# RWKV-6 attention followed by a multiplicative FFN: all tables of a hand-scheduled kernel drawn anew

## The chip, the cores and the metric

The kernel runs on one core of a Trainium2 chip. The metric is the device time of one execution in microseconds (us); lower is better. The engines are named as in the profile: PE (TensorE, matrix products), PEld (its weight loads), DVE (VectorE), ACT (ScalarE), POOL (GpSimd), SP (SyncE, which here only issues transfers).

## The reference

Batch 4, 8 heads, 768 tokens, head size 48; then 3072 tokens of width 384 through a feed-forward block of width 1024 without a nonlinearity beside one product.

```python
state = zeros(B, H, D, D)
for t in range(S):
    cur = einsum('bhd,bhe->bhde', u[None] * k[:, :, t], v[:, :, t])
    y[:, :, t] = einsum('bhd,bhde->bhe', r[:, :, t], state + cur)
    state = w[:, :, t, :, None] * state + einsum('bhd,bhe->bhde', k[:, :, t], v[:, :, t])
x = y.transpose(0, 2, 1, 3).reshape(B * S, H * D)
a, b = x @ w1, x @ w2
out = ((a * b) @ w3) @ w_out
```

All inputs and the output are float32; the kernel's products run in bfloat16.

## The kernel before

**Units.** The 768 tokens are cut into six chunks of 128, the four batches into pairs. A unit is one chunk of one or two batches: units 0 and 1 are one batch each, units 2 to 12 two batches, thirteen in all. The recurrence becomes, inside a chunk, products of 128 x 128 matrices and, between chunks, a state of 48 x 48 per head that is carried along.

**Steps of a unit t.** `ln_t` takes the logarithm of w on ACT, `cs_t` sums it along the tokens (a product with a triangle of ones), `e_t`, `ne_t`, `iw_t` exponentiate it (ACT), `KRk_t`, `rw_t`, `KRr_t` scale k and r with it (DVE). `trk_t` and `trr_t` transpose the scaled k and r on PE (copied out of PSUM by `trke_t`, `trre_t`); units in the sets `DMA_K` and `DMA_R` have the transpose made by a DMA issued from SP instead (`dtk_t`, `dtr_t`). Units in `RAW` transpose the unscaled r (`trw_t`) and sum the logarithms a second time, transposed (`csT_t`, `et_t`, `KRw_t`). `m_t_b` is the score matrix of batch b (L552); it is masked either by one DVE multiplication (`msk_t_b`, L571) or, for the pairs in `POOL_MASK`, copied out by ACT (`mcp_t_b`, L558) and masked in SBUF by POOL or DVE (`maff_t_b`, L566, L564). `kv_t` makes the unit's addition to the state (L638), `T_t`, `S_t`, `Sb_t` carry the state on. `ys_t` is the state's part of y (L587), `yi_t_b` the part inside the chunk (L597). `rk_t`, `ruk_t`, `dg_t`, `dv_t` make the u term, and `yb_t` adds it (L603). `yt_t` transposes y on PE; for units in `DMA_Y` SP issues `dty_t_b` instead.

**Steps of the FFN.** Eight blocks prepare w3 @ w_out once: `wt_f_h` transposes w3 (L373), `w3Te_f` copies it out, `wm_f` multiplies by w_out (L382), `w34e_f` copies the block out. Only two buffers hold the transposed w3, so block f + 2 waits for block f. Then for each unit: `a_t_g` and `b_t_g`, 6 or 12 products into one PSUM bank (L679), `asb_t_g` copies a out (ACT, L684), `abT_t_g` multiplies it by b (DVE, L689), `o_t_b` makes 128 tokens of output (L695), `osb_t_b` copies them out, `st_t_b` stores them.

**Shapes of the products.** Most products on PE use all 128 rows and all 128 columns of the array. `m` and `ys` contract over the padded 64 elements of one head and use 64 rows, two heads taking the two halves in turn. `kv` writes 64 partitions of the output and uses 64 columns.

**Loads.** r, k and v are cast from float32 to bfloat16 by DMAs which POOL issues, in SBUF 192 KB for a unit of two batches (96 KB for one); w is loaded as float32 (384 KB, 192 KB). The weights go the same way: w3 in four parts of 512 KB, w_out (`wo`) 768 KB, w1 and w2 in two parts of 384 KB each. All these stand in POOL's own order, between its arithmetic. SP issues the first two loads of w.

**What sets the order.** Nothing is reordered by a scheduler: `ORDER` lists every step with its engine, and the last loop records them in that order. Each engine runs its own steps strictly in that order; `BANKS` names the PSUM bank and the buffer of each step. `warm7@8` issues eight products of zeros into bank 7; they serve no result.

```python
    with tc.manual_schedule():
        for e in ORDER.split():
            name, _, eng = e.partition("@")
            if name.startswith("warm"):
                warm(int(name[4:]), int(eng))
                continue
            steps[name](eng)
```

Of the kernel before, what the change touches and what calls it, by code (L numbers as in the profile page):

```python
# [48 lines left out]
tk0=0 m0_0=4,5 y0=4,5 yt0=1 kv0=2 a0_0=1 b0_0=0 a0_1=3 b0_1=3 o0_0=0 cs1=2 tr1=2 tk1=1 m1_0=0,1 y1=0,1 yt1=0 kv1=0
a1_0=0 b1_0=2 a1_1=1 b1_1=0 o1_0=4 cs2=4,5 ct2=0,1 tr2=6 tk2=7 m2_0=6,7 m2_1=1,2 y2=3,4 yt2=0 kv2=1 a2_0=5 b2_0=5  # L50
a2_1=2 b2_1=3 a2_2=4 b2_2=2 a2_3=0 b2_3=2 o2_0=5 o2_1=0 cs3=5,6 tr3=1 tk3=4 m3_0=1,2 m3_1=3,4 y3=3,4 yt3=1 kv3=6
a3_0=5 b3_0=0 a3_1=0 b3_1=3 a3_2=4 b3_2=4 a3_3=3 b3_3=0 o3_0=0 o3_1=7 cs4=6,7 tr4=1 tk4=5 m4_0=4,5 m4_1=3,4 y4=5,6
yt4=4 kv4=3 a4_0=0 b4_0=7 a4_1=1 b4_1=4 a4_2=5 b4_2=4 a4_3=1 b4_3=3 o4_0=3 o4_1=7 cs5=1,2 tr5=4 tk5=3 m5_0=1,2
m5_1=2,3 y5=5,6 yt5=4 kv5=7 a5_0=3 b5_0=6 a5_1=2 b5_1=3 a5_2=1 b5_2=3 a5_3=4 b5_3=3 o5_0=3 o5_1=7 cs6=1,2 ct6=6,7
tr6=7 tk6=0 m6_0=0,1 m6_1=2,3 y6=0,1 yt6=2 kv6=0 a6_0=7 b6_0=2 a6_1=7 b6_1=2 a6_2=0 b6_2=4 a6_3=7 b6_3=2 o6_0=4 o6_1=3
cs7=5,6 tk7=2 m7_0=5,6 m7_1=0,1 y7=5,6 kv7=1 a7_0=5 b7_0=1 a7_1=1 b7_1=4 a7_2=0 b7_2=0 a7_3=1 b7_3=0 o7_0=1 o7_1=1
cs8=1,2 tk8=3 m8_0=0,1 m8_1=0,1 y8=5,6 kv8=0 a8_0=2 b8_0=1 a8_1=2 b8_1=4 a8_2=3 b8_2=5 a8_3=4 b8_3=1 o8_0=0 o8_1=6
cs9=5,6 m9_0=2,3 m9_1=3,4 y9=2,3 kv9=0 a9_0=5 b9_0=3 a9_1=2 b9_1=1 a9_2=0 b9_2=3 a9_3=2 b9_3=0 o9_0=5 o9_1=6 cs10=0,1
# [17 lines left out]
trke_1@DVE ruk_0@POOL dg_1@DVE trre_1@ACT KRw_0@DVE w3_1@POOL dg_0@DVE m_1_0@PE cs_2@PE dv_1@POOL mcp_1_0@ACT kv_0@PE
trw_2@PE w3_2@POOL ne_2@ACT csT_2@PE maff_1_0@DVE vin_2@POOL wt_0_1@PE et_2@ACT m_0_0@PE KRk_2@DVE msk_0_0@DVE
trk_2@PE rk_2@POOL pc_2@ACT yi_1_0@PE trke_2@ACT KRw_2@DVE yi_0_0@PE w3Te_0@ACT S_0@DVE dv_0@POOL yb_1@DVE Sb_0@DVE
win_3@POOL yt_1@PE m_2_0@PE m_2_1@PE mcp_2_0@ACT wm_1@PE msk_2_1@DVE w3_3@POOL maff_2_0@POOL yb_0@DVE wm_0@PE
w1_1@POOL wt_3_0@PE w34e_0@ACT yt_0@PE w2_1@POOL wt_3_1@PE xT_1@ACT wt_2_0@PE w3Te_3@DVE wt_2_1@PE rin_3@POOL xT_0@DVE  # L80
wm_3@PE w3Te_2@DVE kin_3@POOL w34e_1@DVE wm_2@PE w34e_3@DVE vin_3@POOL wt_4_0@PE w34e_2@DVE wt_5_0@PE ruk_2@POOL
wt_4_1@PE yi_2_0@PE w3Te_4@DVE wt_5_1@PE kv_2@PE yi_2_1@PE ln_3@ACT S_2@DVE wm_4@PE win_4@POOL dg_2@DVE w3Te_5@ACT
cs_3@PE w1_0@POOL dv_2@DVE iw_3@ACT wm_5@PE e_3@ACT rin_4@POOL yb_2@DVE pc_3@ACT wt_6_0@PE w34e_4@DVE wt_7_0@PE
wt_6_1@PE wt_7_1@PE w3Te_6@DVE yt_2@PE w3Te_7@ACT w2_0@POOL a_0_1@PE xT_2@DVE a_1_1@PE a_2_3@PE b_2_3@PE kin_4@POOL
asb_2_3@ACT a_2_2@PE Sb_2@ACT abT_2_3@DVE asb_0_1@ACT win_5@POOL b_1_1@PE rw_3@DVE asb_1_1@ACT b_2_2@PE ne_3@ACT
KRr_3@DVE trr_3@PE win_6@POOL Sb_1@ACT KRk_3@DVE asb_2_2@ACT b_0_1@PE rk_3@DVE trre_3@ACT trk_3@PE ruk_3@DVE
vin_4@POOL wm_7@PE abT_2_2@DVE trke_3@ACT abT_0_1@DVE m_3_0@PE w34e_5@DVE w34e_7@ACT kv_3@PE kin_5@POOL m_3_1@PE
dg_3@DVE ln_4@ACT wm_6@PE mcp_3_0@ACT T_3@DVE dv_3@POOL msk_3_1@DVE cs_4@PE w34e_6@ACT a_0_0@PE iw_4@ACT rin_5@POOL
a_2_1@PE pc_4@ACT ne_4@ACT rw_4@DVE ys_3@PE vin_5@POOL e_4@ACT a_2_0@PE abT_1_1@DVE maff_3_0@DVE a_1_0@PE asb_2_0@ACT
KRr_4@DVE yi_3_1@PE win_7@POOL asb_1_0@ACT b_2_0@PE asb_0_0@ACT yi_3_0@PE abT_2_0@DVE b_0_0@PE rin_6@POOL KRk_4@DVE  # L90
trr_4@PE asb_2_1@ACT yb_3@DVE trk_4@PE b_1_0@PE rk_4@POOL trke_4@ACT trre_4@DVE b_2_1@PE abT_0_0@DVE ln_5@ACT m_4_0@PE
kin_6@POOL abT_2_1@DVE yt_3@PE mcp_4_0@ACT o_0_0@PE xT_3@DVE abT_1_0@DVE ln_6@ACT maff_4_0@POOL m_4_1@PE cs_5@PE
iw_5@ACT msk_4_1@DVE a_3_0@PE S_3@POOL ne_5@ACT csT_6@PE ruk_4@POOL kv_4@PE pc_6@ACT osb_0_0@ACT o_1_0@PE T_4@DVE
pc_5@ACT e_5@ACT rin_7@POOL dg_4@DVE et_6@ACT a_3_1@PE KRk_5@DVE cs_6@PE kin_7@POOL asb_3_0@ACT rk_5@DVE a_3_3@PE
asb_3_1@ACT rw_5@DVE ys_4@PE win_8@POOL asb_3_3@ACT b_3_3@PE ruk_5@DVE osb_1_0@ACT KRr_5@DVE trk_5@PE ne_6@ACT
abT_3_3@DVE yi_4_1@PE vin_6@POOL trr_5@PE dg_5@DVE kv_5@PE trre_5@ACT yi_4_0@PE o_2_1@PE dv_4@POOL trke_5@DVE ln_7@ACT
T_5@DVE m_5_0@PE dv_5@POOL iw_7@ACT trw_6@PE yb_4@DVE b_3_1@PE Sb_3@ACT yt_4@PE osb_2_1@ACT abT_3_1@DVE win_9@POOL
cs_7@PE mcp_5_0@ACT xT_4@DVE b_3_0@PE KRk_6@DVE pc_7@ACT e_7@ACT rin_8@POOL a_4_3@PE rk_6@DVE ne_7@ACT m_5_1@PE
abT_3_0@DVE a_3_2@PE win_10@POOL asb_4_3@ACT rw_7@DVE trk_6@PE asb_3_2@ACT S_4@DVE a_4_1@PE ln_8@ACT KRw_6@DVE
maff_5_0@POOL b_3_2@PE trke_6@DVE mcp_5_1@ACT vin_7@POOL ys_5@PE rk_7@DVE b_4_0@PE asb_4_1@ACT maff_5_1@DVE yi_5_0@PE  # L100
iw_8@ACT kv_6@PE kin_8@POOL Sb_4@DVE cs_8@PE T_6@DVE yi_5_1@PE abT_3_2@DVE pc_8@ACT b_4_3@PE ln_9@ACT S_5@POOL
yb_5@DVE a_4_0@PE ne_8@ACT vin_8@POOL b_4_1@PE Sb_5@DVE asb_4_0@ACT ruk_7@DVE a_4_2@PE e_8@ACT win_12@POOL ruk_6@DVE
o_3_0@PE abT_4_1@DVE abT_4_3@DVE kin_10@POOL asb_4_2@ACT KRk_7@DVE b_4_2@PE abT_4_0@DVE kv_7@PE m_6_1@PE abT_4_2@DVE
cs_9@PE mcp_6_1@ACT KRk_8@DVE yt_5@PE o_3_1@PE KRr_7@DVE pc_9@ACT ne_9@ACT rw_8@DVE osb_3_0@ACT T_7@DVE rk_8@POOL
trk_7@PE e_9@ACT dg_6@DVE st_3_0@SP m_6_0@PE st_2_1@SP trk_8@PE xT_5@ACT dtr_7@SP o_2_0@PE S_7@DVE trke_8@ACT
# [649 lines left out]
```

## Time and profile before

| | |
|---|---|
| time, 3 runs | 179.97, 180.78, 184.8 us; median 180.78 us |
| the profiled execution | 180.96 us, of which the span is 179.3 us and 1.66 us lie around it |
| busy share | PE 90%, DVE 74%, POOL 59%, ACT 55% |
| granted clock of PE, mean | 0.981 of full speed |
| bytes moved by DMA | 25.08 MB, 140 GB/s over the span |
| the chain that ended last | PE 53%, DVE 19%, DMA 10%, issue 6%, POOL 5%, ACT 3% |

The span runs from the first to the last instruction. The busy shares are averages over three stages: a start in which the weights arrive, a middle in which attention and FFN run beside each other, and an end with FFN alone. In a listing by time a row has the start, the length, the engine, the line and what was written from what; neighbours of one kind are merged (x18 is eighteen instructions). In square brackets stands the idle time before it and what ended that. Products overlap, so the length of a PE row reaches into the next one: what a row costs is the distance to the next row's start.

### The profile page before, as it was taken

What the parts mean: (1) busy time and instruction counts of PE and PEld (TensorE: products, weight loads), DVE (VectorE), ACT (ScalarE), POOL (GpSimd) and SP (SyncE); (2) the same over time, 40 slices, a digit from 0 to 9 for tenths busy, and PEclk for the clock granted to TensorE, in tenths of its full rate; (3) what the DMA queues carried; (4) which work ended last, traced back from release to release, by engine and by line L of the source; (5) the groups of instructions that cost most, each with busy time, mean ns of one, the idle gap of its engine ahead of it and who ended that gap; (6) DMA issues with size and microseconds to landing.
All of it is one profiled execution on the core that took longest, in us unless ns stands there. A gap on an engine that the chain in (4) does not pass through costs nothing.

```text
span 179.3 us, 4622 instructions
## 1 busy us (share of the span) xinstructions
PE 161.1 (90%) x1933; PEld 118.0 (66%) x1933; DVE 133.4 (74%) x207; ACT 98.7 (55%) x161; POOL 105.4 (59%) x99
## 2 busy tenths in 40 slices
...
GB/s 94 162 184 174 211 211 207 177 195 186 214 117 181 65 22 183 125 171 171 42 139 192 131 133 193 68 189 123 139 128 216 142 129 27 84 132 70 4 130 135
DMA packets 100423, 25.08 MB, mean 140 GB/s; under 512 B 92689, under 2 KB 98322, under 8 KB 100402
## 3 DMA queue, kind: packets, MB, share of 16 engines
...
## 4 chain that ended last, share of the span: by engine, by line
PE 53%; DVE 19%; DMA 10%; issue 6%; POOL 5%; ACT 3%; SPq 1%; POOLq 0%; DVEq 0%; ACTq 0%
PE banks L679 24%; PE banks L695 11%; PE banks L382 6%; DMA win<-in_w_dram 4%; DMA vin<-in_v_dram 3%; DMA xT<-yb 3%; PE banks L552 3%; DVE KR L446 2%; DVE KR L487 2%; DVE rk L521 2%; DVE rw L479 2%; PE banks L638 2%; PE banks L597 2%; DVE dg L531 2%; DVE w_bf L689 1%
## 5 line engine op out<-in xcount | busy, mean ns | idle before, releaser
L679 PE MATMUL banks<-xT,w_bf 128*128 128x256 bf16 (+1 forms) x624 | 70.9, 264 | 3.7 <-DMA xT<-yb 1.7
L679 PEld LDWEIGHTS <-w_bf 128*128 128x128 bf16 x624 | 54.7, 98 | 11.9 <-issue 4.7
L684 ACT COPY a_sb<-banks 128x512 f32<-128x512 f32 x48 | 27.8, 593 | 21.7 <-PE banks L679 19.8
L689 DVE TENSOR_TENSOR abT<-a_sb,banks 128x512 bf16<-128x512 f32 x28 | 18.8, 681 | 7.5 <-PE banks L679 6.1
L566 POOL TENSOR_SCALAR_AFFINE_SELECT Mbf<-Mbf 128x1024 bf16<-128x1024 bf16 x10 | 11.3, 1132 | 19.5 <-ACT Mbf L558 19.5
L695 PE MATMUL banks<-w,abT 128*128 128x384 bf16 x112 | 20.3, 326 | 0.0
L558 ACT CAST Mbf<-banks 128x1024 bf16<-128x1024 f32 x14 | 14.2, 1013 | 7.5 <-PE banks L552 7.5
L689 DVE TENSOR_TENSOR w_bf<-a_sb,banks 128x512 bf16<-128x512 f32 x20 | 13.2, 679 | 6.5 <-ACT a_sb L684 4.7
L700 ACT COPY osb<-banks 128x384 f32<-128x384 f32 x16 | 7.7, 481 | 17.7 <-PE banks L695 16.6
L540 POOL TENSOR_TENSOR dv<-vin,dg 128x768 bf16<-128x768 bf16 (+1 forms) x8 | 11.0, 1378 | 8.9 <-DVE dg L531 7.4
L337 POOL DMA_DIRECT2D rin<-in_r_dram x13 | 14.8, 1136 | 0.0
L603 DVE TENSOR_TENSOR yb<-banks,dv 128x768 bf16<-128x768 f32 (+1 forms) x13 | 11.6, 890 | 4.3 <-PE banks L597 3.0
L571 DVE TENSOR_TENSOR Mbf<-banks,mask 128x1024 bf16<-128x1024 f32 x10 | 12.1, 1219 | 3.5 <-PE banks L552 3.5
L337 POOL DMA_DIRECT2D vin<-in_v_dram x13 | 14.7, 1132 | 0.0
L337 POOL DMA_DIRECT2D kin<-in_k_dram x13 | 14.6, 1129 | 0.1
L695 PE MATMUL banks<-w,w_bf 128*128 128x384 bf16 x80 | 14.6, 326 | 0.0
L695 PEld LDWEIGHTS <-abT 128*128 128x128 bf16 x112 | 10.5, 98 | 6.1
L382 PE MATMUL banks<-wo_bf,w3T 128*128 128x384 bf16 x64 | 13.5, 368 | 0.4 <-DVE w3T L377 0.4
L409 ACT ACTIVATE lw<-win 128x768 bf16<-128x768 f32 (+1 forms) x13 | 10.3, 796 | 6.3 <-DMA win<-in_w_dram 6.3
L446 DVE TENSOR_TENSOR KR<-kin,NEt 128x768 bf16<-128x768 bf16 (+1 forms) x13 | 12.8, 994 | 1.0 <-PE banks L638 0.7
L337 POOL DMA_DIRECT2D win<-in_w_dram x11 | 13.1, 1189 | 0.0
L531 DVE TENSOR_REDUCE dg<-ruk 128x16 f32<-128x768 bf16 (+1 forms) x13 | 11.4, 880 | 0.0
...
## 6 DMA issues: line engine op xcount, KB each, us to landing
...
wo_bf<-in_moe_w_out_dram POOLq DMA_DIRECT2D x1, 768.0 KB, 9.6
```

Source lines behind the costliest of these rows:

```text
L337: QUEUE[eng].dma_start(dst, src)
L382: nc.tensor.matmul(one(f"wm{fi}")[:, :DM], lhsT=w3T[fi % 2][:, gi, :], rhs=wo_bf[:, gi, :], start=(gi == 0), stop=(gi == FI - 1))
L446: nc.vector.tensor_mul(KRs[:, 0, :, :D], kk, N_)
L531: nc.vector.reduce_sum(dgs, ruks, axis=AX.X)
L558: copier(eng)(Mbf[bank[f"M{t}_{b}"]], mview())
L566: nc.gpsimd.affine_select(x, x, compare_op=Alu.is_gt, fill=0.0, base=0, channel_multiplier=-1, pattern=[[0, 2 * HP], [1, C]])
L571: nc.vector.tensor_mul(Mbf[bank[f"M{t}_{b}"]], mview(), mask[:, None, None, :].to_broadcast([C, 2, HP, C]))
L603: nc.vector.tensor_add(ybs.rearrange("t b (q e d) -> t e (b q) d", e=2, d=D), yview().rearrange("t e (x d) -> t e x d", d=D), dvs.rearrang ...
L679: nc.tensor.matmul(o[:, f, :], lhsT=wt[:, di, fi * P:(fi + 1) * P], rhs=x[:, di, :T], start=(di == 0), stop=(di == DI - 1))
L684: copier(eng)(a_sb[bank[f"sa{t}_{g}"]], one(f"a{t}_{g}"))
L689: nc.vector.tensor_mul(ab[:, g * per:(g + 1) * per, :T], sa.rearrange("p (f t) -> p f t", t=T), one(f"b{t}_{g}").rearrange("p (f t) -> p f ...
L695: nc.tensor.matmul(one(f"o{t}_{b}")[:, :DM], lhsT=ab[:, fi, b * C:(b + 1) * C], rhs=w34[:, fi, :], start=(fi == 0), stop=(fi == FI - 1))
```

## The change

`ORDER`, `BANKS` and the sets `RAW`, `DMA_R`, `DMA_K` and `POOL_MASK` are all new; no other line of the program differs (it is one line shorter, so line numbers fall by one).

```diff
-RAW = {0, 2, 6}
-DMA_R = {7, 8, 9, 10, 11, 12}
-DMA_K = {9, 10, 11, 12}
+RAW = {1, 2}
+DMA_R = {8, 9, 10, 11, 12}
+DMA_K = {6, 8, 10, 11, 12}
 DMA_Y = {7, 8, 9, 10, 11, 12}
-POOL_MASK = {(1, 0), (2, 0), (3, 0), (4, 0), (5, 0), (5, 1), (6, 1), (7, 0), (8, 1), (9, 0), (9, 1), (10, 0), (10, 1),
-    (11, 1)}
+POOL_MASK = {(2, 0), (4, 0), (5, 1), (6, 1), (7, 1), (8, 0), (9, 0), (9, 1), (11, 1), (12, 0)}
...
-zeros@DVE table@ACT win_1@SP ones@DVE warm5@17 I128@POOL win_0@SP w3_0@POOL u@SP rin_1@POOL kin_0@POOL ln_1@ACT
...
+zeros@DVE table@ACT win_0@SP ones@DVE warm5@7 padlw@DVE mask@POOL win_1@SP w3_1@POOL padkr@DVE u@SP padr@DVE I128@POOL
...
```

Steps that change engine or kind, counted over the two tables:

| | before | now |
|---|---|---|
| products of zeros | 32 in runs of 17, 7, 8 | 28 in runs of 7, 4, 3, 4, 7, 3 |
| masks by one DVE multiplication (`msk`) | 10 | 14 |
| masks through ACT (`mcp`), then POOL / DVE (`maff`) | 14, then 10 / 4 | 10, then 6 / 4 |
| `ruk` on DVE / POOL | 7 / 6 | 11 / 2 |
| `rk` on DVE / POOL | 9 / 4 | 8 / 5 |
| `S` on DVE / POOL | 6 / 5 | 4 / 7 |
| `w3Te` on DVE / ACT | 5 / 3 | 3 / 5 |
| places in PE's order where the shape of the products changes | 77 | 46 |

PE in the stretch around units 6 and 7 (`L695` is `o`, `L679` is `a` or `b`, `L638` `kv`, `L552` `m`, `L425` `cs`, `L587` `ys`, `L597` `yi`; `KR_101`, `KRT_103` and `Sbf_128` belong to unit 6, `KR_102`, `KRT_104` and `Sbf_127` to unit 7; the rows of one step and the full-shape steps between are left out). Before:

```order
L638 MATMUL banks<-vin_83,KR_102 64x48
...
L552 MATMUL banks<-KRT_103 128x128
...
L425 MATMUL banks<-lw_90,LT 128x384
...
L587 MATMUL banks<-Sbf_128,KRT_103 128x48
...
L679 MATMUL banks<-xT_130,w_bf 128x256
...
L597 MATMUL banks<-vin_82,Mbf_108 128x48
...
L587 MATMUL banks<-Sbf_127,KRT_104 128x48
```

Now, one line lower in the file each:

```order
L678 MATMUL banks<-xT_130,w_bf 128x256
...
L637 MATMUL banks<-vin_83,KR_102 64x48
...
L637 MATMUL banks<-vin_82,KR_101 64x48
...
L586 MATMUL banks<-Sbf_128,KRT_103 128x48
...
L586 MATMUL banks<-Sbf_127,KRT_104 128x48
...
L596 MATMUL banks<-vin_82,Mbf_106 128x48
```

`kv` and `ys` of both units stand in one block, where they stood in four places among full-shape products.

POOL near the start (`L363` w3, `L356` w_out, `L337` loads of r, k, v, w, `L525` `ruk`, `L540` `dv`, `L521` `rk`). Before:

```order
L337 DMA win_86<-in_w_dram 128x16x48
L337 DMA vin_76<-in_v_dram 128x8x48
L337 DMA rin_64<-in_r_dram 128x16x48
L337 DMA kin_71<-in_k_dram 128x16x48
L356 DMA wo_bf<-in_moe_w_out_dram 128x8x384
L525 TENSOR_TENSOR ruk_111<-rk_109,u_bc 128x384
L363 DMA w_bf<-in_moe_w_dram 128x2x1024
L540 TENSOR_TENSOR dv_116<-vin_77,dg_114 128x384
L363 DMA w_bf<-in_moe_w_dram 128x2x1024
L337 DMA vin_78<-in_v_dram 128x16x48
L521 TENSOR_TENSOR rk_109<-rin_64,kin_71 128x768
L540 TENSOR_TENSOR dv_115<-vin_76,dg_113 128x384
```

Now:

```order
L336 DMA win_86<-in_w_dram 128x16x48
L336 DMA rin_63<-in_r_dram 128x8x48
L362 DMA w_bf<-in_moe_w_dram 128x2x1024
L355 DMA wo_bf<-in_moe_w_out_dram 128x8x384
L336 DMA kin_71<-in_k_dram 128x16x48
L336 DMA rin_64<-in_r_dram 128x16x48
L362 DMA w_bf<-in_moe_w_dram 128x2x1024 x2
L336 DMA vin_77<-in_v_dram 128x8x48
L336 DMA vin_78<-in_v_dram 128x16x48
L336 DMA win_87<-in_w_dram 128x16x48
L520 TENSOR_TENSOR rk_109<-rin_64,kin_71 128x768
```

The second part of w3 stands ahead of w_out, r and k of unit 2 behind it, and POOL's arithmetic on units 0 and 1 no longer stands between the loads.

## Rows read from the trace of the kernel before

**Rows 1.** The page's head: busy time and share of the span.
```profile
span 179.3 us, 4622 instructions
PE 161.1 (90%) x1933; PEld 118.0 (66%) x1933; DVE 133.4 (74%) x207; ACT 98.7 (55%) x161; POOL 105.4 (59%) x99
```

**Rows 2.** Busy time by stretch: length, engines, granted PE clock, DMA share, GB/s.
```profile
0.00:24.80 24.80, 17.46 (x168) 9.77 (x168) 15.64 (x38) 10.96 (x19) 19.97 (x27) 0.95 1.50 168
24.80:40.20 15.40, 14.88 (x149) 9.78 (x148) 9.70 (x15) 5.31 (x9) 14.60 (x14) 0.86 1.70 197
40.20:65.00 24.80, 23.55 (x346) 18.82 (x344) 19.30 (x29) 19.32 (x33) 15.59 (x14) 1.00 1.57 139
65.00:110.00 45.00, 41.85 (x575) 32.28 (x574) 43.55 (x63) 34.91 (x58) 32.15 (x27) 1.00 1.43 141
110.00:154.00 44.00, 41.96 (x545) 31.77 (x542) 36.45 (x52) 20.06 (x31) 23.11 (x19) 1.00 0.97 129
154.00:175.40 21.40, 21.36 (x162) 15.59 (x160) 8.76 (x15) 7.67 (x15) 0.00 (x0) 1.00 0.28 93
```

**Rows 3.** Listing by time of PE, in the start.
```profile
1.25 5.82 PE L320 MATMUL banks<-zeros 128*128 128x512 bf16 x17 [1.25 <-DVE zeros L255]
...
20.96 0.62 PE L513 MATMUL banks<-I,KR 128*128 128x128 bf16 x8 [2.94 <-DVE KR L446]
...
24.82 4.91 PE L382 MATMUL banks<-wo_bf,w3T 128*128 128x384 bf16 x16
...
31.20 2.77 PE L382 MATMUL banks<-wo_bf,w3T 128*128 128x384 bf16 x16 [0.41 <-DVE w3T L377]
```

**Rows 4.** Listing by time of PE: full-shape products before half-array ones, and others.
```profile
134.96 0.40 PE L552 MATMUL banks<-KRT 64*128 64x128 bf16 x8
135.29 0.83 PE L679 MATMUL banks<-xT,w_bf 128*128 128x256 bf16 x6
...
139.06 0.62 PE L552 MATMUL banks<-KRT 64*128 64x128 bf16 x16
...
144.20 2.13 PE L679 MATMUL banks<-xT,w_bf 128*128 128x256 bf16 x18
146.26 0.37 PE L587 MATMUL banks<-Sbf,KRT 64*128 64x48 bf16 x16
...
156.30 2.13 PE L679 MATMUL banks<-xT,w_bf 128*128 128x256 bf16 x18
158.27 1.46 PE L695 MATMUL banks<-w,abT 128*128 128x384 bf16 x8
159.57 6.71 PE L679 MATMUL banks<-xT,w_bf 128*128 128x256 bf16 x60
```

**Rows 5.** Transfers: sizes and median time from issue to landing.
```profile
wo_bf<-in_moe_w_out_dram POOLq DMA_DIRECT2D x1, 768.0 KB, 9.6
```

**Rows 6.** Listing by time of POOL, in the start.
```profile
11.76 0.93 POOL L356 DMA_DIRECT2D wo_bf<-in_moe_w_out_dram  x1
...
19.65 0.83 POOL L540 TENSOR_TENSOR dv<-vin,dg 128x384 bf16<-128x384 bf16 x1
```

**Rows 7.** Listing by time of DVE, at the same place and at 45 us.
```profile
17.55 3.35 DVE L446 TENSOR_TENSOR KR<-kin,NEt 128x768 bf16<-128x768 bf16 x1
...
45.11 0.56 DVE L446 TENSOR_TENSOR KR<-kin,NEt 128x768 bf16<-128x768 bf16 x1 [0.24 <-ACT NEt L442]
```

**Rows 8.** Groups by line: busy time, mean ns, idle before and what ended it.
```profile
L571 DVE TENSOR_TENSOR Mbf<-banks,mask 128x1024 bf16<-128x1024 f32 x10 | 12.1, 1219 | 3.5 <-PE banks L552 3.5
L566 POOL TENSOR_SCALAR_AFFINE_SELECT Mbf<-Mbf 128x1024 bf16<-128x1024 bf16 x10 | 11.3, 1132 | 19.5 <-ACT Mbf L558 19.5
L525 DVE TENSOR_TENSOR ruk<-rk,u_bc 128x768 bf16<-128x768 bf16 x6 | 3.2, 551 | 0.0
L525 POOL TENSOR_TENSOR ruk<-rk,u_bc 128x768 bf16<-128x768 bf16 x5 | 8.2, 1649 | 0.0
L377 DVE COPY w3T<-banks 128x1024 bf16<-128x1024 bf16 x5 | 3.4, 687 | 4.3 <-PE banks L373 4.2
```

More of the change, by code (lines that the diff above doesn't have):

```diff
@@ L49 @@
[L49 to L58, printed above, removed]
@@ L76 @@
[L76 to L85, printed above, removed]
@@ L86 @@
[L86 to L105, printed above, removed]
@@ new lines @@
+iw_0@ACT win_2@POOL wt_3_0@PE wt_2_0@PE rin_1@POOL csT_1@PE cs_0@PE wt_3_1@PE ne_0@ACT wt_2_1@PE w3_0@POOL warm7@3
+e_0@ACT pc_0@ACT pc_1@ACT wo@POOL KRk_0@DVE rw_0@DVE kv_0@PE uc@DVE warm7@4 kin_2@POOL rk_0@DVE KRk_1@DVE KRr_0@DVE
+S_0@DVE trr_0@PE rin_2@POOL trk_0@PE trre_0@ACT warm7@7 trke_0@DVE et_1@ACT ruk_0@DVE w3_2@POOL rk_1@DVE ln_2@ACT
+dg_0@DVE w3_3@POOL Sb_0@DVE ruk_1@DVE cs_2@PE dv_0@DVE csT_2@PE vin_1@POOL warm7@3 pc_2@ACT ne_2@ACT vin_2@POOL
+et_2@ACT m_0_0@PE wt_1_0@PE msk_0_0@DVE wt_0_0@PE win_3@POOL wt_1_1@PE trw_1@PE trk_1@PE wt_0_1@PE KRw_1@DVE yi_0_0@PE
@@ new lines @@
+w3Te_0@ACT trke_1@DVE w3Te_1@DVE m_1_0@PE msk_1_0@DVE wm_1@PE wm_0@PE KRk_2@DVE w3Te_3@ACT yb_0@DVE w34e_1@DVE
+trk_2@PE rk_2@POOL w3Te_2@ACT trw_2@PE wm_3@PE KRw_2@DVE trke_2@ACT w2_1@POOL m_2_0@PE w34e_3@DVE kin_3@POOL m_2_1@PE
+mcp_2_0@ACT yt_0@PE msk_2_1@DVE wt_4_0@PE wt_5_0@PE wt_4_1@PE rin_3@POOL wt_5_1@PE wm_2@PE w3Te_5@DVE ruk_2@DVE
+maff_2_0@DVE wt_7_0@PE w3Te_4@ACT wm_5@PE dg_1@DVE dg_2@DVE dv_1@POOL wt_7_1@PE wm_4@PE w34e_2@DVE w3Te_7@ACT
+w1_1@POOL w34e_5@DVE w1_0@POOL dv_2@DVE w34e_0@ACT yi_2_0@PE yi_1_0@PE vin_3@POOL yi_2_1@PE wt_6_0@PE xT_0@DVE
@@ new lines @@
+ln_3@ACT wm_7@PE yb_1@DVE yb_2@DVE w2_0@POOL wt_6_1@PE win_5@POOL cs_3@PE w3Te_6@DVE yt_1@PE ne_3@ACT kv_1@PE xT_1@DVE
+kv_2@PE win_4@POOL S_1@DVE yt_2@PE w34e_4@ACT wm_6@PE pc_3@ACT KRk_3@DVE iw_3@ACT rin_4@POOL xT_2@DVE Sb_1@DVE
+trk_3@PE rk_3@DVE w34e_6@ACT b_2_3@PE e_3@ACT ruk_3@DVE b_0_1@PE S_2@DVE trke_3@ACT rw_3@DVE b_1_1@PE dg_3@DVE
+w34e_7@ACT b_2_2@PE KRr_3@DVE a_1_1@PE a_2_3@PE asb_1_1@ACT a_2_2@PE abT_1_1@DVE asb_2_3@ACT a_0_1@PE asb_2_2@ACT
+dv_3@POOL trr_3@PE abT_2_2@DVE asb_0_1@ACT a_1_0@PE trre_3@ACT abT_0_1@DVE a_2_0@PE kin_4@POOL abT_2_3@DVE asb_1_0@ACT
@@ new lines @@
+b_3_2@PE rw_6@DVE rin_9@POOL pc_6@ACT osb_1_0@ACT ne_6@ACT m_5_1@PE abT_3_2@DVE yt_4@PE vin_7@POOL mcp_5_1@ACT cs_7@PE
+rk_7@DVE KRk_6@DVE o_3_1@PE xT_4@ACT rin_8@POOL ruk_7@DVE dtk_6@SP KRr_6@DVE e_7@ACT a_4_2@PE rw_7@DVE pc_7@ACT
+ne_7@ACT maff_5_1@DVE trr_6@PE osb_3_1@ACT KRr_7@DVE m_5_0@PE ys_5@PE ln_8@ACT st_3_1@SP msk_5_0@DVE S_4@POOL a_4_0@PE
+st_1_0@SP asb_4_2@ACT trr_7@PE kin_8@POOL asb_4_0@ACT dg_7@DVE yi_5_1@PE b_4_3@PE trre_7@ACT vin_6@POOL KRk_7@DVE
+yi_5_0@PE cs_8@PE ln_9@ACT yb_5@DVE a_4_3@PE rin_12@POOL Sb_5@ACT trre_6@DVE trk_7@PE asb_4_3@ACT o_3_0@PE Sb_4@DVE
```

116 lines of the change are left out of this document (68 added, 48 removed).

## The prediction

> **What bounds the kernel now.** I read the page's head first, then the busy time by stretch, then the listings by time of PE, POOL and DVE. The head shows PE busy for 161.1 of 179.3 us, DVE for 133.4 and POOL for 105.4 [rows 1]: no order can win more than PE's idle 18.2 us unless PE's own work shrinks. The stretches show where the idle time lies [rows 2]. Up to 24.8 us PE is busy 17.46 us, but much of that is products of zeros (the first seventeen alone last 5.82 us [rows 3]); PE then waits for loads and for unit 2, the longest time 2.94 us [rows 3]. From 24.8 to 40.2 us PE is busy 14.88 of 15.40, at a granted clock of 0.86. From 40.2 to 175.4 us, 135.2 us, it is busy 23.55 + 41.85 + 41.96 + 21.36 = 128.7, so it waits 6.5 us in many small pieces. In the middle of this, 65 to 110 us, DVE is busy 43.55 of 45 and PE 41.85 of 45: both are nearly full. After 154 us PE alone is full. So the path is a start set by loads, then PE, with DVE close behind it in the middle.
>
> **Changes of shape.** The part of the change that needs no luck is PE's own work. Eighteen full-shape products ahead of `ys` last 146.26 - 144.20 = 2.06 us to the next start; the same eighteen ahead of another full-shape step last 158.27 - 156.30 = 1.97 [rows 4]. Going into the half-array shape costs 0.09 us. For the way out, eight score products reach the next full-shape start after 135.29 - 134.96 = 0.33 us, and eight more of them add 0.62 - 0.40 = 0.22 [rows 4], so 0.11 us of the 0.33 is the way out. I take 0.10 a change. The order has 77 such changes before and 46 now. Up to the first product with w1 or w2 there are 12 before and 10 now; in the start PE waits anyway, so these two count for nothing. In the body it is 65 against 36: 29 x 0.10 = **-2.9 us**. This counts in full only where PE is the limit.
>
> **Other products.** Unit 6 leaves `RAW`: eight 128-column products go and eight one-column ones come, about -0.3 us by the distances in the listing. Transposes trade places between PE and the DMA: unit 9's k and unit 7's r come to PE, k of units 6 and 8 leave it, and unit 6 transposes its scaled r instead of its raw one. PE has as many transposes as before, so these cancel. **-0.3 us** in all. The four products of zeros that go stood in front of waits; nothing for them.
>
> **The start.** The first product with w_out begins at 24.82 us [rows 3] behind unit 2's scores, which themselves waited for DVE. In the new order it stands ahead of unit 2 and needs w_out, one copied w3 block and the scores of unit 1 ahead of it. w_out was issued at 11.76 us [rows 6] and landed 9.6 us later [rows 5], at 21.4. Up to and with w_out POOL's queue held 2,624 KB before and holds 2,656 now (w3 part 512, w 384, `wo` 768 and six to ten small loads of 96 to 192 before; two w3 parts and five small loads now), and the page's GB/s in these stretches, 168 and 197 [rows 2], say that the transfers, not POOL's issuing, set the rate. So w_out lands at about 21.4 again, a little later for the larger queue: I take a start at 21.7, 3.1 us earlier. At that point the new order has done less real work: unit 2's transposes and scores and some small steps are still to come, four transposes of w3 more are done; by distances in PE's listing the difference is 1.3 us. That leaves -1.8. Next, the sixteen w_out products at 24.82 last 4.91 us and the sixteen at 31.20 last 2.77 [rows 3]: the first ran at the lower of PE's two clock levels, after the wait of 2.94 us, and lost 2.1 us. The new order leaves a wait of about the same size ahead of w_out (I put the end of unit 1's scores near 19 us, an estimate from its loads and steps), but PE does more ahead of it; the loss is between none and 2.1, nothing shows which, and I take half: -1.0. Start: **-2.8 us**, with bounds of 0 (w_out later by the jitter of a transfer, clock as before) and -3.9.
>
> **DVE and POOL.** Four more masks are DVE multiplications at 1.22 us, +4.9; four more `ruk` at 0.55 (one of them half size), +2.0; two w3 copies fewer at 0.69, -1.4; two `S`, one `rk` and one w34 copy fewer at about the 0.55 of a step of that size, -2.2; the rest cancels [rows 8]. DVE: +3.3. POOL loses four masks at 1.13 and four `ruk` at 1.65 (one half size) and takes one `rk`, two `S`: about -6.4 [rows 8]. ACT loses four mask copies and takes as much in w3 and transpose copies. DVE's 3.3 us is hidden where it has idle time, up to 40 us and after 110, but between 65 and 110 us it has 1.45 us left [rows 2]. What PE saves there by fewer changes it may have to wait for DVE: of the 29 saved changes about eleven lie in this stretch. I give back **+1.0 us**, with bounds of 0 and the 3.3 of the whole.
>
> DVE's times hold waits for POOL. `KR` took 3.35 us at 17.55, while POOL ran `rk` and then `dv`, to 20.48, and 0.56 at 45.11 [rows 6, 7]. The Trainium skill, in SBUF: State Buffer (section "SBUF: two separate sides"), says that a port pair which DVE and GpSimd share is an exclusive lock, held for the whole instruction. The row agrees. By that rule POOL's 6.4 us less of arithmetic would shorten DVE by some 2 us, nothing would be given back, and the time would be 1.0 us less than my sum.
>
> **The sum.** Against the profiled execution's 180.96 us (span 179.3 [rows 1] and 1.66 around it): 180.96 - 2.9 - 0.3 - 2.8 + 1.0 = **176.0 us**. The median of the three runs, 180.78, stands 0.2 below this execution, so the gain is 2.6% of it. 2% is 3.6 us, about what a measurement of this kernel can tell from no change: faster means below 177.2, slower above 184.4. The forecast's own spread, 174 to 178, has about a seventh above 177.2.
>
> **Rivals.**
> *A. The waits go too.* The new table may also halve PE's 6.5 us of waits after 40 us: 176.0 - 3.3 = 172.7. For it: most are single waits of under 1.3 us on DVE, which other neighbours would fill. Against: DVE has more work, not less. 15%.
> *B. DVE sets the pace.* In the old trace DVE is busy 133.4 - 8.8 = 124.6 of the first 154 us [rows 1, 2] and so idle 29.4; its last sum `yb` ends there. With 3.3 more and the same idle time the attention ends at 157.3. Behind it stand now 18 FFN groups and six output steps instead of 16 and nine; at 1.97 / 3 = 0.66 a group [rows 4] and 159.57 - 158.27 = 1.30 an output step [rows 4] that is 19.6 us against 22.2. So 1.66 + 179.3 + 3.3 - 2.6 gives 181.7 us. For it: 65 to 110 us. Against: DVE's idle time before 40 us came from the start, which shortens. 17%.
> *C. The clock stays low in the start.* Seven products of zeros stand where seventeen did, and waits lie between the short runs. If two runs of sixteen w_out products go at the lower level, 4.2 us are lost where I have 1.1: 179.1. The Trainium skill, in TensorE: Matmul & The Clock Gate (Part 1), says that the lower level is the default and that activity lifts it; the 4.91 against 2.77 agrees, and by that rule alone 179.1 would be the result. Against: the run of w_out products is itself long. 12%.
> *D. Slower: POOL holds DVE up in the middle.* As B, and two steps of DVE's full stretch meet POOL's arithmetic like the one of 3.35 us, at 2.8 us each [rows 7]: 181.7 + 5.6 = 187.3. It decides once DVE's waits grow by more than 2.7 us over B. For it: three more steps of `rk` and `S` on POOL. Against: 6.4 us less of POOL in all. 6%.
> That the shorter list of changes is not real is excluded by PE's order.
>
> **Numbers.** Forecast 50%, A 15%, B 17%, C 12%, D 6%. Faster: 0.43 of the forecast and A, 0.58. Within 2%: 0.07, B and C, 0.36. Slower: D, 0.06. The range reaches from A's side with the clock's gain, 171.5, to B at 181.7; D lies outside, and some of the spread below A and above B.
>
> **What would show it.** PE's busy time down by about 3 us without more idle in the body; `kv` and `ys` rows in blocks; the first w_out product near 21.7 us and its sixteen at 2.8 to 4.9 us; DVE busy near 137 us. Wrong if PE's idle time after the start exceeds 8 us, if w_out lands after 23 us, or if DVE is full from 60 us on.

## The result and the profile after

The changed kernel takes **168.6 us** (median of four runs, 167.96 to 169.13) against 180.47 of the kernel before on the same chip: ratio 0.935, 95% interval 0.930 to 0.940. Times are medians of all executions of a kernel; ratios, and the gains and losses worked out from them, compare the fast executions alone, so that a median with slow ones in it can lie above its ratio. Forecast were 176.0 us and a range of 171.5 to 181.7: the direction was right, but the time lies below the range, and the gain of 11.9 us is 2.4 times the forecast one. Lines of the new kernel are one lower than before (L678 is `a` or `b`); in the experiments' kernels one or two lower.

The page's head, which answers to [rows 1]:

```profile
span 167.4 us, 4611 instructions
PE 155.9 (93%) x1928; PEld 118.0 (70%) x1929; DVE 127.1 (76%) x210; ACT 98.3 (59%) x161; POOL 100.1 (60%) x94
```

PE is busy 5.2 us less. DVE was to be busy for about 137 us and is busy for 127.1. That is the first sign of the step that failed. Busy time by stretch, as in [rows 2], cut at the first product with w_out and at the first with w1 or w2:

```profile
0.00:19.85 19.85, 16.19 (x129) 8.79 (x130) 9.68 (x34) 8.74 (x16) 15.86 (x23) 1.00 1.39 166
19.85:37.07 17.22, 16.77 (x207) 11.83 (x207) 14.19 (x25) 10.05 (x14) 12.44 (x12) 1.00 1.73 190
37.07:65.00 27.93, 27.93 (x439) 23.67 (x437) 25.25 (x40) 24.30 (x39) 21.71 (x19) 1.00 1.99 186
65.00:110.00 45.00, 42.55 (x564) 33.04 (x564) 41.67 (x62) 33.83 (x59) 35.04 (x30) 0.96 1.63 151
110.00:140.00 30.00, 28.82 (x397) 22.98 (x388) 25.39 (x37) 13.56 (x22) 13.92 (x11) 1.00 1.10 144
140.00:163.50 23.50, 23.50 (x216) 17.66 (x213) 10.93 (x17) 7.38 (x14) 1.09 (x1) 1.00 0.25 77
```

Behind 37 us PE now idles 2.45 + 1.18 = 3.6 us, where it idled 6.5 before. The listing of PE shows the places ([rows 3] for the start):

```profile
19.85 2.77 PE L381 MATMUL banks<-wo_bf,w3T 128*128 128x384 bf16 x16 [0.20 <-DVE w3T L376]
22.46 0.61 PE L512 MATMUL banks<-I,KR 128*128 128x128 bf16 x8
...
36.62 0.61 PE L512 MATMUL banks<-I,KR 128*128 128x128 bf16 x8 [0.45 <-DVE xT L625]
37.07 1.10 PE L678 MATMUL banks<-xT,w_bf 128*128 128x256 bf16 x11
...
95.15 0.43 PE L637 MATMUL banks<-vin,KR 128*64 128x48 bf16 x16 [2.30 <-DVE w_bf L688]
...
96.20 5.52 PE L678 MATMUL banks<-xT,w_bf 128*128 128x256 bf16 x36
```

The first w_out product starts at 19.85 us instead of 24.82 and runs at the upper clock level (2.77 us for sixteen). w_out was issued at 9.59 us and landed 10.0 us later:

```profile
9.59 0.97 POOL L355 DMA_DIRECT2D wo_bf<-in_moe_w_out_dram  x1
```

```profile
wo_bf<-in_moe_w_out_dram POOLq DMA_DIRECT2D x1, 768.0 KB, 10.0
```

The first product with w1 or w2 starts at 37.07 instead of 40.20, and ahead of it stands more real work than before: `wm_6` and `wm_7` (sixteen products, at 22.46 - 19.85 = 2.61 us for sixteen) and unit 3's first transposes (0.45).

One long wait is left, 2.30 us at 92.85. Behind it the granted clock is 0.50 from 96 to 99 us, the lower level, and the 36 products there last 5.52 us, where 18 take 2.13 at the upper level [rows 4]: some 1.3 us more. That belongs to this execution and not to the order. In a second profile of the same program (`a_same`) the same wait of 2.30 us is followed by a clock of 1.00:

```profile
95.90 4.31 PE L678 MATMUL banks<-xT,w_bf 128*128 128x256 bf16 x36
```

There PE idles 4.4 us behind 37 us instead of 3.6. The groups by line of DVE show its steps on bf16 operands in SBUF. Before:

```profile
L446 DVE TENSOR_TENSOR KR<-kin,NEt 128x768 bf16<-128x768 bf16 x11 | 12.2, 1110 | 1.0 <-PE banks L638 0.7 <-ACT NEt L442 0.2
L487 DVE TENSOR_TENSOR KR<-rw,Et 128x768 bf16<-128x768 bf16 x9 | 8.0, 893 | 0.0
L521 DVE TENSOR_TENSOR rk<-rin,kin 128x768 bf16<-128x768 bf16 x7 | 6.2, 892 | 0.0
```

And after:

```profile
L445 DVE TENSOR_TENSOR KR<-kin,NEt 128x768 bf16<-128x768 bf16 x11 | 7.6, 694 | 1.1 <-DMA kin<-in_k_dram 1.0
L486 DVE TENSOR_TENSOR KR<-rw,Et 128x768 bf16<-128x768 bf16 x10 | 6.1, 614 | 0.0
L520 DVE TENSOR_TENSOR rk<-rin,kin 128x768 bf16<-128x768 bf16 x6 | 3.3, 548 | 0.0
```

The same operation on the same shape takes 1110 ns on average in one kernel and 694 in the other, and 550 where nothing disturbs it. With `rw` (782 and 651), `ruk` (551 and 621) and `dv` (951 and 1108), steps times excess over 550 (951 for `dv`) give 13.7 us before and 4.5 after. The difference of 9.2, less the 3.3 us of more work that was forecast, is 5.9: DVE's busy time fell by 6.3.

### The profile page after: what moved, and what is told of

It reads as the page before. It is cut to its first block, busy times and chain, and to the rows that moved or that the text cites. A ratio compares the mean times of both kernels' runs of the same rounds, so it can differ in the third digit from the quotient of the medians.

```text
span 167.4 us, 4611 instructions
## 1 busy us (share of the span) xinstructions
PE 155.9 (93%) x1928; PEld 118.0 (70%) x1929; DVE 127.1 (76%) x210; ACT 98.3 (59%) x161; POOL 100.1 (60%) x94
## 4 chain that ended last, share of the span: by engine, by line
PE 60%; DMA 15%; DVE 10%; POOL 7%; SPq 3%; issue 3%; ACT 0%; POOLq 0%; DVEq 0%
PE banks L678 34%; PE banks L694 15%; DMA rin<-in_r_dram 7%; DMA kin<-in_k_dram 6%; PE banks L551 3%; DMA xT<-yb 2%; DVE KR L445 2%; SPq L611 2%; POOL kin L336 2%; PE banks L596 2%; PE banks L512 1%; PE banks L637 1%; PE banks L424 1%; DVE yb L602 1%; POOL rin L336 1%
## 5 line engine op out<-in xcount | busy, mean ns | idle before, releaser
L678 PE MATMUL banks<-xT,w_bf 128*128 128x256 bf16 (+1 forms) x624 | 70.0, 267 | 0.8 <-DMA xT<-yb 0.7
L678 PEld LDWEIGHTS <-w_bf 128*128 128x128 bf16 x624 | 56.3, 99 | 8.6 <-DMA xT<-yb 1.0
L570 DVE TENSOR_TENSOR Mbf<-banks,mask 128x1024 bf16<-128x1024 f32 x14 | 17.1, 1219 | 3.0 <-PE banks L551 2.8
L520 POOL TENSOR_TENSOR rk<-rin,kin 128x768 bf16<-128x768 bf16 x5 | 8.2, 1638 | 15.3 <-DVE ruk L524 7.9
L441 ACT ACTIVATE NEt<-banks 128x768 bf16<-128x768 f32 (+1 forms) x13 | 10.1, 774 | 5.4 <-PE banks L429 4.3
L445 DVE TENSOR_TENSOR KR<-kin,NEt 128x768 bf16<-128x768 bf16 (+1 forms) x13 | 8.3, 642 | 6.5 <-ACT NEt L441 5.4
L381 PE MATMUL banks<-wo_bf,w3T 128*128 128x384 bf16 x64 | 11.6, 326 | 0.2 <-DVE w3T L376 0.2
```

The costliest lines, as they stand in the source:

```text
L381: nc.tensor.matmul(one(f"wm{fi}")[:, :DM], lhsT=w3T[fi % 2][:, gi, :], rhs=wo_bf[:, gi, :], start=(gi == 0), stop=(gi == FI - 1))
L445: nc.vector.tensor_mul(KRs[:, 0, :, :D], kk, N_)
L570: nc.vector.tensor_mul(Mbf[bank[f"M{t}_{b}"]], mview(), mask[:, None, None, :].to_broadcast([C, 2, HP, C]))
L678: nc.tensor.matmul(o[:, f, :], lhsT=wt[:, di, fi * P:(fi + 1) * P], rhs=x[:, di, :T], start=(di == 0), stop=(di == DI - 1))
```

## The experiments

Ratios are to the kernel before, run on the same chip each time.

**One part alone: the start, the body, one held step.** `h_head` has the new order up to the first w1 or w2 product and the old one behind it; `h_body` the reverse; `b_rk2` is the kernel before with two steps on another engine:

```
b_rk2:  rk_2@POOL -> rk_2@DVE    dv_0@POOL -> dv_0@DVE
```

> The start of the changed kernel (all its steps ahead of trk of unit 3, with its banks and its kinds of step for units 0 to 2), then the remaining steps in the order of the kernel before. If the gain adds up from the two traces (5.3 us of start, 6.6 us of body): 175 us. If the start only matters together with the new body: 178 or more.

> The start of the kernel before (all its steps ahead of the first product with w1), then the remaining steps in the changed kernel's order. If the gains add up: 174 us. If the body's gain needs the new start (loads and DVE work done earlier): 177 or more.

> The kernel before, with two steps of the start moved from POOL to DVE and nothing else: rk of unit 2 and dv of unit 0. POOL theory (in the start, POOL's arithmetic held KR of unit 2 on DVE for 2.8 us, and PE's order stood behind it): KR of unit 2 takes 0.6 to 1.2 us instead of 3.35, the first w_out product starts near 22 us instead of 24.8, PE keeps the higher clock there, and the time falls by 3 to 5 us, to 175.5 to 177.5. Load theory (the start is set by the order of the loads): KR may be shorter, but the time stays within 1 us of before.

Measured: `h_head` 180.78 us (0.989, 0.982 to 0.997), `h_body` 175.84 (0.972, 0.962 to 0.982), `b_rk2` 178.24 (0.987, 0.977 to 0.997). In `h_head` the first w_out product comes at 20.01 us, as in the changed kernel, but the old body gives the lead back, first to a load that the new start issues later (the part of w1 that is loaded first, issued at 29.86 us instead of 26.64):

```profile
20.01 2.77 PE L380 MATMUL banks<-wo_bf,w3T 128*128 128x384 bf16 x16 [0.20 <-DVE w3T L375]
...
37.89 4.37 PE L677 MATMUL banks<-xT,w_bf 128*128 128x128 bf16 x56 [1.55 <-DMA w_bf<-in_moe_w_dram]
```

The two halves give 1.1% and 2.8% alone and 6.5% together. The traces show which half leans on the other. In `h_body` the stretch from the first w1 or w2 product to PE's last step takes 126.1 us (44.12 to 170.2), as in the changed kernel (126.4) and against 135.2 before: the new body does not need the new start. What `h_body` lacks is the start, which reaches that product at 44.12 us, with `wm_6`, `wm_7` and unit 3's transposes done. In `h_head` the same stretch takes 136.8 us, although it has this work no longer to do: the new start is worth little without the new body.

`b_rk2` frees unit 2's `KR` (on DVE), and PE's wait of 2.94 us ahead of its transposes [rows 3] goes:

```profile
17.75 0.56 DVE L444 TENSOR_TENSOR KR<-kin,NEt 128x768 bf16<-128x768 bf16 x1
```

```profile
18.37 0.62 PE L511 MATMUL banks<-I,KR 128*128 128x128 bf16 x8 [0.15 <-DVE KR L444]
...
21.81 0.34 PE L620 MATMUL banks<-I,yb 128*128 128x128 bf16 x3 [1.90 <-DVE yb L601]
...
23.05 3.96 PE L380 MATMUL banks<-wo_bf,w3T 128*128 128x384 bf16 x16
...
37.21 1.00 PE L677 MATMUL banks<-xT,w_bf 128*128 128x128 bf16 x15
```

A new wait of 1.90 us (for `yb`, behind DVE's extra steps) takes part of it, yet the first w1 or w2 product comes 2.99 us earlier, at 37.21. The sixteen w_out products took 3.96 us, so the clock did not stay at its upper level as I had expected. By the ratio the gain is 2.3 us (0.5 to 4.1), less than the 3 to 5 forecast.

**The price of a change of shape.** `t_thin` and `t_full` put 23 products of zeros into the end, between the steps of the stretch where only PE works:

```
t_full: matmul(bank, lhsT=zeros[:128, :128], rhs=zeros[:128, :64])
t_thin: matmul(bank, lhsT=zeros[:64, :128],  rhs=zeros[:64, :64])
```

> The changed kernel with 23 extra products of zeros, 64 columns each, put singly between the full-shape steps of the end, where PE alone is full; they contract over 64 rows, so each one brings two changes of shape. To be compared with the twin that contracts over 128 rows. Theory (0.10 us a change): 46 x 0.10 = 4.6 us longer than the twin. Rival (a change costs nothing): the same time as the twin.

> The changed kernel with the same 23 extra products of 64 columns at the same places, contracting over 128 rows: no change of shape. Each is 64 columns at 2.4 GHz, 0.027 us: at least 0.6 us more than the changed kernel, 169.2 to 170; the twin with 64 rows is dearer by what 46 changes of shape cost.

Measured: 175.20 us (0.965, 0.956 to 0.974) and 169.84 (0.938, 0.932 to 0.943). First and last rows of PE's listing, `t_full`:

```profile
143.50 0.19 PE L719 MATMUL banks<-zeros 128*128 128x64 bf16 x1
143.53 0.81 PE L679 MATMUL banks<-xT,w_bf 128*128 128x256 bf16 x6
144.18 0.19 PE L719 MATMUL banks<-zeros 128*128 128x64 bf16 x1
...
162.46 1.47 PE L695 MATMUL banks<-w,w_bf 128*128 128x384 bf16 x8
```

The same of `t_thin`:

```profile
145.33 0.20 PE L719 MATMUL banks<-zeros 64*128 64x64 bf16 x1
145.46 0.83 PE L679 MATMUL banks<-xT,w_bf 128*128 128x256 bf16 x6
146.22 0.20 PE L719 MATMUL banks<-zeros 64*128 64x64 bf16 x1
...
169.00 1.47 PE L695 MATMUL banks<-w,w_bf 128*128 128x384 bf16 x8
```

From the first extra product to the last step it is 162.46 - 143.50 = 18.96 us and 169.00 - 145.33 = 23.67. The difference is 4.71 us for 46 changes: **0.102 us each**, 0.13 - 0.03 = 0.10 of it behind the thin product and 0.11 ahead of it (0.76 against 0.65). The busy time of one product does not show it (0.20 against 0.19): it lies between their starts. The Trainium skill, in TensorEngine Tiling (Array Packing) (Key Properties), says that changing the tiling mode drains TensorE; the rows fit that and give a price. It is the price of going from 128 rows to 64 and back; `kv`, with 128 rows and 64 columns, was not priced by itself.

**Shapes alone, in both directions.** `a_split` exchanges fifteen neighbouring pairs of PE's steps in the changed kernel (46 changes become 76), `b_swap` moves PE's steps of the kernel before by at most three places (77 become 52); all other engines' orders stand. Two of the pairs of `a_split`:

```
- a_2_0@PE m_3_1@PE      + m_3_1@PE a_2_0@PE
- b_3_3@PE m_4_1@PE      + m_4_1@PE b_3_3@PE
```

> The changed kernel with fifteen neighbouring pairs of PE's steps in the body exchanged (by at most three places), so that PE changes its product shape 76 times instead of 46; every other engine's order, every engine and every load place as in the changed kernel. Theory (a change of shape costs PE 0.10 us and PE is the limit): +30 x 0.10 = 3.0 us on the changed kernel's 168.6, PE's busy time about 3 us up, its idle time within 1 us of before: about 171.6, ratio to the kernel before about 0.95. Rival (shape costs nothing beyond the moved place; the gain came from waits alone): within 0.7 us of 168.6, PE's busy time unchanged.

> The kernel before with PE's steps in the body moved by at most three places so that its 77 changes of shape become 52; every other engine's order, every engine and load place as before. Theory (the shape's price of 0.10 us holds, and it was saved together with the waits by one search): 25 x 0.10 = 2.5 us less work of PE, but the half-shape steps now stand in twos and threes and ask DVE, ACT and POOL for their masks at once, so PE's waits grow by as much or more: 178 to 184 us. Rival (the new order's gain is its grouping of shapes): 175 or less.

Measured: `a_split` 173.39 us (0.959, 0.952 to 0.966), by the ratios 4.3 us above the changed kernel, of which 30 x 0.102 = 3.1 us are the shapes: from the first w1 or w2 product on PE is busy 124.9 us against 121.6 in `a_same`, both at a clock of 1.00. PE's waits there also grew, from 4.4 to 6.3 us, the longest new one 1.68 us for a transpose by DMA. That I expected them unchanged was wrong. `b_swap` took 195.40 us (1.067, 1.057 to 1.077): 12 us slower with 25 changes fewer, and worse than either theory had it. PE waits 16.9 us behind the start instead of 6.5. Some of these waits, from PE's listing:

```profile
51.89 0.38 PE L585 MATMUL banks<-Sbf,KRT 64*128 64x48 bf16 x16 [1.39 <-DVE Mbf L569]
...
64.79 0.43 PE L636 MATMUL banks<-vin,KR 128*64 128x48 bf16 x16 [1.39 <-DVE Mbf L569]
...
94.21 0.40 PE L550 MATMUL banks<-KRT 64*128 64x128 bf16 x8 [2.26 <-ACT osb L698]
...
145.78 0.40 PE L550 MATMUL banks<-KRT 64*128 64x128 bf16 x8 [1.78 <-ACT a_sb L682]
```

Each is a score or state step that now waits for DVE or ACT to copy a PSUM bank out. Regrouping PE's steps alone loses here; why the changed kernel's own groups do not lose was not tested apart; on this reading they stand where the banks are free. Two further runs point the same way. `b_group`, an earlier and wider regrouping (in units 4 and 12 some `yi` products came ahead of the `ys` that starts the bank, so that their part of the sum is lost), took 205.43 us (1.125, 1.115 to 1.136). `a_best` regrouped the changed kernel's own steps from 46 to 40 changes:

> The kernel before with PE's steps in the body regrouped by small moves (none by more than six places) so that the 77 changes of shape become 51; the order of every other engine and all engines and load places as before. Theory: PE's busy time falls by 26 x 0.10 = 2.6 us; where PE waits for DVE in the middle, part of it turns into waiting: time 178 to 179.5, ratio 0.985 to 0.993. Rival (the new order's gain is shape alone): the whole 12 us would need far more than 0.10 a change, ratio below 0.96. Other rival (no price): ratio 1.00 or above, PE busy unchanged.

> The changed kernel with ruk of unit 9 and S of unit 7 moved from POOL to DVE (as in the run that took the wait of 2.3 us away) and PE's steps of the body regrouped by small moves from 46 changes of shape to 40. Theory: 6 x 0.10 = 0.6 us below the 166.9 of that run, 165.5 to 166.8, ratio 0.915 to 0.925. Rival (PE waits more where it was regrouped): 167 or more.

`a_best` took 172.48 us (0.954, 0.948 to 0.960) instead of 165.5 to 166.8: six changes saved, and new waits of 1.37, 1.32 and 1.11 us ahead of `m` steps. The rival was right.

**POOL's hold on DVE.** A hold is meant where a DVE step lasts longer than its shortest instance while POOL works; the profile books that time as DVE's busy time and not as a wait. `a_dum` adds 17 multiplications on POOL that nobody needs; `a_eng` keeps the new order but puts `rk`, `ruk`, `dv` and `S` back on the engines of before (nineteen steps); `b_eng` is the kernel before with the new engines for the same nineteen:

```
a_dum:  rin_4@POOL + 3 x tensor_mul(scratch, u_bc, u_bc)@POOL   (4 after rk_10, 4 after vin_12, 6 at the end)
a_eng:  ruk_0 ruk_2 ruk_4 ruk_11 ruk_12 rk_4 dv_0 dv_4 dv_8 S_9: DVE -> POOL
        ruk_6 rk_11 rk_12 dv_7 dv_11 dv_12 S_4 S_6 S_7: POOL -> DVE
```

> The changed kernel with seventeen extra bf16 multiplications of 128x768 on POOL, of 1.64 us by the rows of the same operation, on a buffer that nobody reads: three in POOL's idle time at 36.9 us, four at 96.5, four at 122.5, six after its last step at 141.6, where DVE does only sums that read a bank and copies of banks. Theory (a POOL operation on SBUF holds DVE's bf16 steps with operands in SBUF alone): KR, rw, rk and ruk of DVE in the first three stretches go from 0.55 to between 1 and 2 us, DVE's busy time rises by 6 to 9 us, PE waits for it, the time rises by 2 to 5 us; in the end stretch abT and osb stay at 0.69 and 0.55 and nothing is lost. Rival (DVE's steps became shorter in the changed kernel for a reason of their own order): DVE's steps stay at 0.55 and the time within 0.7 us of 168.6.

> The changed kernel's order, banks and load places, but rk, ruk, dv and S of every unit on the engine that had them before (nineteen steps change engine: five ruk, two dv... to POOL; S and three others back to DVE). Theory (part of the gain is that POOL holds DVE less because these steps were taken from it): DVE's KR, rw, rk means rise from 0.55 to 0.7 towards 0.8 to 0.9 and the time to 171 to 174. Rival (the order alone, not the engines, keeps POOL's and DVE's steps apart): means unchanged, time 168 to 170.

> The kernel before, in its own order, with nineteen steps (rk, ruk, dv and S of some units) on the engine that the changed kernel gives them: ten from POOL to DVE, nine from DVE to POOL. Theory (what counts is which POOL step meets which DVE step in time, so engines are worth something only together with an order made for them): 178 to 183, DVE's KR and rw means stay above 0.75. Rival (the engines alone take POOL's hold off DVE): DVE's busy time at or below 128 and the time at 173 to 176.

`a_dum`: 175.73 us (0.974, 0.969 to 0.979), 7.1 above the changed kernel, more than forecast; DVE is busy 136.6 us, 9.5 more, and PE waits 8.6 us behind the start instead of 3.6. That POOL's own later steps came later is not the reason that shows: DVE waits 0.7 us for POOL's `dv` (0.6 in the changed kernel), PE for no load behind the start. POOL's and DVE's listings in the first stretch:

```profile
37.62 4.99 POOL L720 TENSOR_TENSOR scr<-u_bc 128x768 bf16<-128x768 bf16 x3
```

```profile
37.67 1.88 DVE L521 TENSOR_TENSOR rk<-rin,kin 128x768 bf16<-128x768 bf16 x1
39.59 1.70 DVE L525 TENSOR_TENSOR ruk<-rk,u_bc 128x768 bf16<-128x768 bf16 x1
41.21 0.54 DVE L651 TENSOR_TENSOR Sst<-banks,pc 128x384 f32<-128x384 f32 x1
41.68 1.35 DVE L479 TENSOR_TENSOR rw<-rin,iw 128x768 bf16<-128x768 bf16 x1
```

`rk` and `ruk` took 0.54 and 0.56 us at this place in the changed kernel, `rw` 0.55. `Sst`, which reads a bank, keeps its length (0.55 there). So do such steps at the end, where POOL ran six more in one go, from 148 to 157 us:

```profile
147.87 9.20 POOL L720 TENSOR_TENSOR scr<-u_bc 128x768 bf16<-128x768 bf16 x6
```

```profile
151.76 0.69 DVE L689 TENSOR_TENSOR abT<-a_sb,banks 128x512 bf16<-128x512 f32 x1 [0.42 <-PE banks L679]
```

The Trainium skill, in SBUF — State Buffer (SBUF: two separate sides), has the lock held for a whole instruction, on DVE's side only by a step with two inputs in SBUF or in a two-port mode; both stretches agree.

`a_eng`: 177.66 us (0.984, 0.977 to 0.991), 9 us above the changed kernel with the same shapes, the same PE order and POOL busy 101.7 us instead of 100.1. It is more than its theory's 171 to 174. DVE is busy 134.3 us instead of 127.1, and PE waits 9.9 us behind the start. `dv` and the second `KR` are now the held ones; a `dv` of 3.08 us at 82.91, beside POOL's `rk`, stands ahead of a PE wait of 2.40 us:

```profile
L485 DVE TENSOR_TENSOR KR<-rw,Et 128x768 bf16<-128x768 bf16 x10 | 8.7, 879 | 0.5 <-DMA KRT<-KR 0.3 <-ACT Et L481 0.2
L538 DVE TENSOR_TENSOR dv<-vin,dg 128x768 bf16<-128x768 bf16 x5 | 7.6, 1520 | 0.0
```

`b_eng`: 187.70 us (1.038, 1.029 to 1.048): the new engines in the old order make it slower, and the first `KR` stays at 1010 ns. But DVE is busy 131.4 us, 2.0 less than before, so more time held in all is not what lost here. PE's waits behind the start grow from 6.5 to 11.0 us, the longest 3.56 us for a transpose of y by DMA. A `KR` of 3.42 us at 104.14, beside POOL's `dv` and `ruk`, stands in the chain that ended last; how much of the loss is its own was not tested. So the choice of engines has no price of its own. It depends on the order which POOL step meets which DVE step, and on whether PE is waiting for that step.

**The last long hold.** In the changed kernel the wait of 2.30 us stands behind this on DVE and POOL:

```profile
91.28 2.12 DVE L445 TENSOR_TENSOR KR<-kin,NEt 128x768 bf16<-128x768 bf16 x1
93.32 1.18 DVE L524 TENSOR_TENSOR ruk<-rk,u_bc 128x768 bf16<-128x768 bf16 x1
```

```profile
91.30 1.67 POOL L524 TENSOR_TENSOR ruk<-rk,u_bc 128x768 bf16<-128x768 bf16 x1
92.90 1.18 POOL L653 TENSOR_TENSOR Sst<-Tst,pc 128x384 f32<-128x384 f32 x1
```

```
a_ruk9, a_ruk9b:  ruk_9@POOL -> ruk_9@DVE    S_7@POOL -> S_7@DVE
```

> The changed kernel with ruk of unit 9 and S of unit 7 on DVE instead of POOL, at the same places. POOL theory: KR of unit 8, which took 2.12 us beside POOL's ruk, takes 0.55 to 1.0, PE's wait of 2.3 us at 92.8 us goes or shrinks below 0.8, the stretch at the lower clock behind it goes, and the time falls by 1.5 to 3.5 us, to 165 to 167. Rival (DVE is simply full there, and gets 1.1 us more): same time or up to 1 us slower.

> The changed kernel itself, beside the next one on the same chip: 168.6, ratio 0.935.

> The changed kernel with ruk of unit 9 and S of unit 7 moved from POOL to DVE, once more beside the changed kernel itself. Theory (the wait of 2.3 us and the stretch of lower clock behind it are gone for good): 1.5 to 3 us below the changed kernel. Rival (the earlier difference was chance): within 0.7 us of it.

The first run gave 166.86 us (0.922, 0.911 to 0.933). Beside the changed kernel on one chip, five rounds each: 166.53 us (0.9195, 0.914 to 0.926) against 168.90 (0.934, 0.929 to 0.939). **This version beats both kernels**, the changed one by 2.4 us. DVE's listing at the same place, and the page's head:

```profile
90.08 0.55 DVE L444 TENSOR_TENSOR KR<-kin,NEt 128x768 bf16<-128x768 bf16 x1
90.55 0.55 DVE L523 TENSOR_TENSOR ruk<-rk,u_bc 128x768 bf16<-128x768 bf16 x1
```

```profile
PE 154.2 (94%) x1928; PEld 116.9 (71%) x1929; DVE 125.0 (76%) x212; ACT 98.4 (60%) x161; POOL 97.3 (59%) x92
```

DVE has two steps more and is busy 2.1 us less than in the changed kernel. PE's wait is gone, and behind the start PE idles 1.8 us. The clock is 1.00 in this profile, but so it is in that of `a_same`, where PE idles 4.4 us: the gain is the wait's and not the clock's.

## Why the prediction was too careful, step by step

| step | forecast, us | measured, us |
|---|---|---|
| changes of shape, 29 fewer in the body | -2.9 | -3.0 (29 x 0.102, worked out) |
| other products | -0.3 | not measured apart |
| the start | -2.8 | -6.2 (3.13 earlier, with 3.06 more work done) |
| PE's waits behind the start | +1.0 | -2.8 (6.5 to 3.6; 4.4 in `a_same`) |
| lower clock behind the 2.30 us wait, in this execution | none | +1.3 |
| not accounted for, other products among it | | -1.2 |
| sum of the span | -5.0 | -11.9 |

- **Shapes**: right in size and mechanism, with `kv`'s changes taken at the same price. What the forecast did not say is that saving them can cost more than it brings: `b_swap` lost 12 us.
- **DVE and POOL is the step that failed.** The count of the work was right (+3.3 us), but it was costed as if the time that POOL holds DVE stayed. In the forecast itself `KR` at 3.35 and 0.56 us stood side by side [rows 7]; the excess over all such steps, 13.7 us, could have been added up from the groups by line and was not. The rule gave 2 us, taken from POOL's total; `a_eng` shows that the total says little (POOL's nearly unchanged, 9 us lost). The sign was wrong: nothing was given back, and the waits fell by 2.8 us, outside the bounds stated for them (0 to +3.3). Rival A had nearly this (+1.0 - 3.3 = -2.3), for another reason, that other neighbours would fill the waits. That POOL's holds on DVE make PE wait is shown in both directions (`b_rk2` and `a_ruk9b` take a hold away, `a_dum` and `a_eng` add some); that each of the old waits went for this reason is argued and not shown.
- **The start was mis-sized by 3.4 us**, and its -6.2 lies outside its bounds of 0 and -3.9. I let w_out land at 21.4 us, arguing that the transfers and not POOL's issuing set the rate. It was issued at 9.59 instead of 11.76 and landed 10.0 us later, at 19.6: with slightly more bytes ahead of it, the landing followed the issue. The lower clock was gone as a whole, not half (2.77 for the first sixteen). And unit 2's `KR`, for which PE waited 2.94 us, was POOL's hold too: `b_rk2` brings the first w1 or w2 product forward by 2.99 us by moving two steps off POOL. The forecast's row for this hold agrees with the lock only in part: `KR` began at 17.55, before POOL's `rk` at 18.05, while POOL was still issuing a load.
- **Rivals B, C and D** did not come about in the changed kernel. `a_eng` comes nearest to B and D: with the old engines the new order waits for DVE in the middle, and yet stays below both at 177.66. That C did not show is in part luck. In the profiles of `a_split`, `t_thin` and `a_ruk9`, which have the changed kernel's start, the clock was 0.50 in a part of the stretch from 7 to 15 us, longest in `a_ruk9`, where the first w_out product came at 21.46. Its sixteen ran at the upper level (2.77) there too.
- **What stays open**: the -1.2 us, and how much of the start's 6.2 us is which of its three causes (w_out's earlier issue, the clock, unit 2's `KR`).
